# Float16 halves for the last v product, with a power of two for each token, and the last weights decoded on four engines

## The chip, the cores and the metric

The kernel runs on one core of a Trainium2 chip. The metric is the time of one execution on the device in microseconds (us). Engines are named as in the profile: PE is TensorE (PEld its weight loads), DVE is VectorE, ACT is ScalarE, POOL is GpSimd, SP is SyncE, which issues the DMAs.

## The reference, cut to what matters

Three stages follow one another over 8 batches of 576 tokens with 512 features: a linear attention, a Fourier mixing with a feed-forward network (the main part below), and a channel mixing with its own weights (the last part). The change concerns the last one:

```python
xk = mu_k * x + (1.0 - mu_k) * x_prev      # x_prev: the token before, zeros at a batch's start
xr = mu_r * x + (1.0 - mu_r) * x_prev
k = np.maximum(xk @ w_k, 0.0)              # 512 -> 1024
v = k * k @ w_v                            # 1024 -> 512
r = 1.0 / (1.0 + np.exp(-(xr @ w_r)))      # 512 -> 512
return (r * v).astype(np.float32)
```

The weights come in as float64, in pairs of 32-bit words.

## The kernel before, in words

**Products in halves.** An operand of a large matmul is split into a high and a low part, and a product is three matmuls into one PSUM bank: high by high, high by low, low by high. In most products the parts are float16, scaled by powers of two; in the v product of the last part they are fp32r (32 bits).

**Main part (loop at L896 and on).** The 4608 tokens go in nine blocks of 512. For each of 16 slices f of the hidden layer, `mm1` makes 12 matmuls into one of two `h` banks (L913), ACT takes relu into `hh` (L918), DVE the rest into `hl` (L919), and `mm2`, two slices behind, adds 12 matmuls into four `acc` banks (L933). Between the matmuls `side()` advances generators: attention, the transform and the normalisation of later blocks, and, when these have ended, `last_strand`.

**Preparing the last weights (`last_weights`, L670).** w_r, w_k and w_v are read in pieces of 128x256 float64 numbers (`load_weight`, L150, issued on SP into three `raw` buffers). A first pass over w_r and w_k (24 pieces) finds each matrix's largest magnitude: ACT takes the absolute value of the upper 16 bits (L694), DVE the maximum (L695). Then a reduction over the partitions on POOL (L698) and a few tiny DVE operations give a power of two for each matrix. The second pass goes over all 40 pieces: `decode` (L153) puts float32 numbers together from the words, in three DVE operations (L157 to L159, two `dec` buffers), ACT writes the high part and DVE the low one (L724, L725 for w_r and w_k, float16; L727, L728 for w_v, fp32r). w_v goes first.

**The last part (L963 and on).** For each of nine blocks: r = 4 x 12 matmuls with the mixed tokens as weights (L975), a sigmoid on ACT (L976); then for each of 8 slices f `mmk` makes 12 matmuls (L986), k squared is made in four operations (ACT L990, DVE L991, ACT L992, DVE L993), and `mmv`, two slices behind (three in the last block), adds 12 matmuls into four `acc` banks (L1001). At the end DVE multiplies the sigmoid with the sums (L1022) and SP stores. `mix` (L766) makes the mixed tokens of the next block meanwhile, on ACT and DVE (L781 to L787), after `bound` (L745) has found a scale for the block from its largest value.

**What sets the order.** Each engine runs its instructions in a fixed order, and so does each DMA queue. The order is set when the program is built: a planner walks the written program, with earlier lines first where two could start, and starts in its own time line whatever is ready and has a buffer. So work written late can stand early in a queue: in the profile the first `bound` runs at 870 us, beside block 6 of the main part, though its lines come after that of the last weights.

Of the kernel before, what the change touches and what calls it, by code (L numbers as in the profile page):

```python
# [45 lines left out]
def net(ctx, tc, q, k, v, w1, w2, mu_k, mu_r, w_k, w_v, w_r, ce_d, se_d, cs_d, ss_d, alt_d, id_d, out):  # L46
    nc = tc.nc
# [622 lines left out]
    def last_weights():  # L670

        wp = W["pool"] = back_pools.enter_context(tc.tile_pool(name="wp", bufs=1))
        ts = nc.vector.tensor_scalar
# [4 lines left out]

        top = wp.tile([128, 4], F32, name="top")
        am = wp.tile([128, 2, 16], F32, name="am")  # L680
# [4 lines left out]
        nc.vector.tensor_reduce(out=top[:, 2:3], in_=ab[:, :, 0], axis=AX.XY, op=ALU.max)  # L685
# [11 lines left out]
        nc.vector.tensor_reduce(out=top[:, 0:2], in_=am, axis=AX.X, op=ALU.max)  # L697
        nc.gpsimd.partition_all_reduce(out_ap=top[:, 0:3], in_ap=top[:, 0:3], channels=128, reduce_op=bass_isa.ReduceOp.max)  # L698
        yield 0
        W["top"] = top  # L700

        pw = W["pw"] = wp.tile([128, 4], F32, name="pw")
        scaled = False
        for name, src, nt, n in (plan[2], plan[0], plan[1]):
            f16 = name != "wv"
            if f16 and not scaled:
                m, inv, big_ = pw[:, 0:2], pw[:, 2:4], top[:, 0:2]
                mi, ii, bi = m.bitcast(U32), inv.bitcast(U32), big_.bitcast(U32)
                ts(out=big_, in0=big_, scalar1=LEAST, scalar2=None, op0=ALU.max)
                ts(out=mi, in0=bi, scalar1=3, scalar2=0x3F800000, op0=ALU.logical_shift_left, op1=ALU.bitwise_and)  # L710
                nc.vector.scalar_tensor_tensor(out=mi, in0=bi, scalar=0x40000000, in1=mi, op0=ALU.bitwise_and, op1=ALU.bitwise_or)
                ts(out=ii, in0=mi, scalar1=0x7F800000, scalar2=None, op0=ALU.bitwise_xor)
                ts(out=inv, in0=inv, scalar1=2.0 ** 11, scalar2=None, op0=ALU.mult)
                scaled = True
            h = wp.tile([128, nt, n], F16 if f16 else F32R, name=name + "h")
            l = wp.tile([128, nt, n], F16 if f16 else F32R, name=name + "l")
            W[name] = h, l
            for t in range(nt):
                for c in range(n // 256):
                    cs = slice(256 * c, 256 * c + 256)  # L720
                    x = decode(wp, load_weight(wp, src, t, c, RAW))
                    if f16:
                        s = pw[:, 2 + (name == "wk"):3 + (name == "wk")]
                        nc.scalar.activation(out=h[:, t, cs], in_=x, func=AF.Copy, scale=s)  # L724
                        nc.vector.scalar_tensor_tensor(out=l[:, t, cs], in0=x, scalar=s, in1=h[:, t, cs], op0=ALU.mult, op1=ALU.subtract)  # L725
                    else:
                        nc.scalar.activation(out=h[:, t, cs], in_=x, func=AF.Copy)  # L727
                        nc.vector.tensor_tensor(out=l[:, t, cs], in0=x, in1=h[:, t, cs].bitcast(F32), op=ALU.subtract)  # L728
                    yield 0
# [15 lines left out]
    def bound(i):  # L745
# [11 lines left out]
        ts(out=z[:, 1:2], in0=z[:, 0:1], scalar1=W["top"][:, 2:3], scalar2=LEAST, op0=ALU.mult, op1=ALU.max)  # L757
# [201 lines left out]
    kk = big.tile([128, 2, 4, 512], F32R, tag="w1h", name="kk")  # L959
# [176 lines left out]
```

## Time and profile before

| what | us |
|---|---|
| median of 3 runs | 1589.28 |
| lowest and highest run | 1588.1, 1591.85 |
| the profiled execution | 1591.17 |
| its span, first to last instruction | 1589.4 |
| scans of the last weights (L694) | 873 to 904 |
| decodes of the last weights (L157) | 904 to 1001 |
| the last part's matmuls | 1104.4 to 1585.6 |

PE is busy 93% of the span, DVE 58%, ACT 38%, POOL 10%. In the rows below, a group of instructions stands with its line, engine, operation, "out<-in" tiles, shapes and count; then busy time in us and the mean time of one in ns; then the engine's idle time in front of them and what ended it. "acc", "h" and "side" are PSUM banks.

### The profile page before, as it was taken

How to read it: one execution, taken by the hardware profiler on the slowest of the kernel's cores; microseconds unless marked ns; L12 is line 12 of the kernel's file. 1: busy time of each engine (PE TensorE's matmuls, PEld its weight loads, DVE VectorE, ACT ScalarE, POOL GpSimd, SP SyncE). 2: the span in 40 equal slices, each digit the busy share in tenths (PEclk: the TensorE clock that was granted, in tenths of full speed). 3: DMA queues.
4: the chain of work that ended last, by engine and by line, in shares of the span. 5: the costliest groups of instructions: out<-in, count | busy, mean ns of one | idle time of the engine just before them, and what ended most of it. 6: DMA issues, size and time to landing. Idle time of an engine off the chain costs nothing.

```text
span 1589.4 us, 18119 instructions
## 1 busy us (share of the span) xinstructions
PE 1470.3 (93%) x7072; PEld 827.7 (52%) x7072; DVE 926.5 (58%) x1680; ACT 598.1 (38%) x1034; POOL 163.6 (10%) x121
## 2 busy tenths in 40 slices
PE   4647795899999999999999889999999999999999
PEld 3534553554555555555555334444555655565555
DVE  5898977636647557465463698531455445444532
ACT  4555543323223333232232433321444334433532
POOL 0034432211020010110100120000000000000000
PEclk9878997899999999999999999999999999999999
DMA  9834422101202011011010533100011001100000
GB/s 358 298 126 172 149 99 73 47 2 46 73 23 82 16 47 59 16 48 59 15 53 20 174 126 113 47 27 27 27 54 53 27 27 53 54 27 27 27 27 27
DMA packets 44867, 112.30 MB, mean 71 GB/s; under 512 B 5708, under 2 KB 12013, under 8 KB 43757
## 3 DMA queue, kind: packets, MB, share of 16 engines
q1 hardware_dynamic: 44780, 111.14, 20.0%
q8 instruction: 55, 0.90, 0.2%
q14 instruction: 32, 0.25, 0.0%
HBM read 92.25 MB, written 18.87 MB: 70 GB/s over the span
## 4 chain that ended last, share of the span: by engine, by line
PE 74%; DVE 15%; DMA 5%; issue 2%; ACT 2%; POOL 2%; SPq 0%; DVEq 0%; ACTq 0%; POOLq 0%
PE acc L933 17%; PE h L913 17%; PE acc L1001 13%; PE h L986 12%; PE h L975 6%; DMA raw<-in_w_k_dram 3%; PE side L495 2%; PE side L515 2%; DMA raw<-in_w_dram 1%; PE side L416 1%; DVE words L239 1%; PE side L363 1%; DVE hl L919 1%; DVE dec L159 1%; DVE m L322 1%
## 5 line engine op out<-in xcount | busy, mean ns | idle before, releaser
L913 PE MATMUL h<-unh,w1h 128*128 128x512 f16 (+1 forms) x608 | 226.3, 373 | 14.0 <-DVE hl L919 8.6
L913 PE MATMUL h<-unh,w1l 128*128 128x512 f16 (+1 forms) x608 | 224.5, 371 | 5.3 <-POOL w1l L257 5.3
L913 PE MATMUL h<-unl,w1h 128*128 128x512 f16 (+1 forms) x608 | 225.9, 372 | 1.2 <-DVE unl L658 1.2
L933 PE MATMUL acc<-hl,w2h 128*128 128x512 f16 x576 | 219.3, 381 | 2.6 <-DVE hl L919 2.6
L933 PE MATMUL acc<-hh,w2l 128*128 128x512 f16 x576 | 219.3, 381 | 0.0
L933 PE MATMUL acc<-hh,w2h 128*128 128x512 f16 x576 | 212.1, 382 | 4.3 <-ACT hh L918 4.3
L1001 PE MATMUL acc<-wvh,kk 128*128 128x512 f32 x576 | 202.9, 416 | 0.0
L913 PEld LDWEIGHTS <-w1h 128*128 128x128 f16 x1216 | 118.6, 99 | 145.1 <-issue 17.2
L919 DVE SCALAR_TENSOR_TENSOR hl<-h,hh 128x512 f16<-128x512 f32 x144 | 98.9, 688 | 157.7 <-ACT hh L918 156.7
L933 PEld LDWEIGHTS <-w2h 128*128 128x128 f16 x1152 | 111.9, 98 | 136.1 <-issue 6.9
L986 PE MATMUL h<-x,wkh 128*128 128x512 f16 x576 | 173.0, 380 | 0.0
L918 ACT ACTIVATE hh<-h 128x512 f16<-128x512 f32 x144 | 84.9, 591 | 192.3 <-PE h L913 192.1
L991 DVE SCALAR_TENSOR_TENSOR ke<-h,ke 128x512 f32<-128x512 f32 x72 | 49.6, 688 | 141.9 <-ACT ke L990 141.9
L1001 PEld LDWEIGHTS acc<-wvh,kk 128*128 128x128 f32 x576 | 108.6, 189 | 30.1
L1001 PE MATMUL acc<-wvl,kk 128*128 128x512 f32 x288 | 113.5, 394 | 0.0
L986 PE MATMUL h<-x,wkl 128*128 128x512 f16 x288 | 109.2, 379 | 0.0
L990 ACT ACTIVATE ke<-h,z 128x512 f32<-128x512 f32 x72 | 49.2, 683 | 140.8 <-PE h L986 140.8
L913 PEld LDWEIGHTS <-w1l 128*128 128x128 f16 x608 | 59.9, 99 | 72.3 <-POOL w1l L257 7.3
L933 PEld LDWEIGHTS <-w2l 128*128 128x128 f16 x576 | 56.6, 98 | 67.3 <-issue 4.9
L986 PEld LDWEIGHTS <-wkh 128*128 128x128 f16 x576 | 52.7, 98 | 70.5 <-issue 14.0
L975 PE MATMUL h<-wrh,x 128*128 128x512 f16 x288 | 88.6, 380 | 0.0
L787 DVE TENSOR_TENSOR x<-aa,x 128x512 f16<-128x512 f32 x72 | 47.9, 686 | 61.0 <-PE h L975 52.4
(330 smaller groups left out, 2251.4 us busy)
## 6 DMA issues: line engine op xcount, KB each, us to landing
raw<-in_w_dram SPq DMA_DIRECT2D x22, 512.0 KB, 3.9
vt<-in_v_dram SPq DMA_DIRECT2D x16, 650.0 KB, 5.2
kt<-in_k_dram SPq DMA_DIRECT2D x16, 576.0 KB, 4.0
qt<-in_q_dram SPq DMA_DIRECT2D x16, 576.0 KB, 4.2
out_dram<-oo SPq DMA_DIRECT2D x36, 256.0 KB, 2.1
y<-yT SPq DMA_DIRECT2D x8, 1026.0 KB, 5.0
w2h<-in_w_dram SPq DMA_DIRECT2D x8, 1024.0 KB, 6.8
w2l<-in_w_dram SPq DMA_DIRECT2D x8, 1024.0 KB, 8.5
```

What stands on the lines that cost most here:

```text
L495: mm(out=pt, lhsT=a[:, e, g, js], rhs=c[:, g, :], start=first, stop=(e == 1 and g == 1 and a is el))
L515: mm(out=pt, lhsT=a[:, i, cols], rhs=c[:, i, :], start=(i == 0 and c is ch and a is yh), stop=False)
L787: nc.vector.tensor_tensor(out=l[:, t, 0:n], in0=a, in1=h[:, t, 0:n], op=ALU.subtract)
L913: mm(out=pt[:, o:o + m], lhsT=a[:, t, fs], rhs=c[:, t, o:o + m], start=(t == 0 and a is w1h and c is xh), stop=(t == 3 and a is w1l))
L918: nc.scalar.activation(out=hh[:, 0:n], in_=pt[:, 0:n], func=AF.Relu)
L919: nc.vector.scalar_tensor_tensor(out=hl[:, 0:n], in0=pt[:, 0:n], scalar=0.0, in1=hh[:, 0:n], op0=ALU.max, op1=ALU.subtract)
L933: mm(out=acc[x][:, 0:n], lhsT=a[:, f, xs], rhs=c[:, 0:n], start=(f == 0 and a is w2h and c is hh), stop=(f == NF - 1 and a is w2l))
L975: mm(out=pt[0:m, :], lhsT=a[:, t, o:o + m], rhs=c[:, t, :], start=(t == 0 and a is rh and c is wrh), stop=(t == 3 and a is rl))
L986: mm(out=pt[:, 0:n], lhsT=a[:, t, fs], rhs=c[:, t, 0:n], start=(t == 0 and a is wkh and c is kh), stop=(t == 3 and a is wkl))
L990: nc.scalar.activation(out=kr[:, 0:n], in_=pt[:, 0:n], func=AF.Relu, scale=z[:, 5:6])
L991: nc.vector.scalar_tensor_tensor(out=kr[:, 0:n], in0=pt[:, 0:n], scalar=0.0, in1=kr[:, 0:n], op0=ALU.max, op1=ALU.mult)
L1001: mm(out=acc[x][0:m, :], lhsT=a[:, o:o + m], rhs=c[:, f, :], start=(f == 0 and a is h2 and c is wvh), stop=(f == NFK - 1 and a is l2))
```

## The change

1. In `decode`, ACT shifts the low word down by 29 bits (a multiplication by 2^-29, in place), DVE does two operations in place of three, and POOL adds the two.
2. w_v is scanned as well (16 pieces more in the first pass), gets a power of two, becomes float16, and is decoded last. A `yield` more stands between decoding and splitting.
3. `mix` for k adds up the squares of the mixed tokens (four ACT squares, two POOL adds, one DVE operation into bf16). `token_scale`, after the second of the four r groups, adds them over the partitions with one matmul of a ones matrix, and makes from the sum a power of two for each token, `G`, and its inverse `rb`. `token_descale`, behind the first k group, turns `rb` by four matmuls of one column, and gives a factor for each token, `dd`.
4. k squared: DVE relu times `G`, ACT square, ACT copy to float16, DVE the rest in float16. The last multiply also takes `dd`.
5. The two halves of a mixed tile lie in one tile. For k these alternate between two places.

```diff
@@ decode
+        nc.scalar.activation(out=lo, in_=lo, func=AF.Copy, scale=2.0 ** -29)
         nc.vector.tensor_scalar(out=x, in0=hi, scalar1=3, scalar2=0x3FFFFFFF, op0=ALU.logical_shift_left, op1=ALU.bitwise_and)
-        nc.vector.scalar_tensor_tensor(out=x, in0=lo, scalar=29, in1=x, op0=ALU.logical_shift_right, op1=ALU.bitwise_or)
         nc.vector.scalar_tensor_tensor(out=x, in0=hi, scalar=0xC0000000, in1=x, op0=ALU.bitwise_and, op1=ALU.bitwise_or)
+        nc.gpsimd.tensor_tensor(out=x, in0=x, in1=lo, op=ALU.add)
@@ last_weights
-        for w, (name, src, nt, n) in enumerate(plan[0:2]):
+        for w, (name, src, nt, n) in enumerate(plan):
...
+        ones_ = W["onesb"] = wp.tile([128, 128], BF16, name="onesb")
+        nc.vector.memset(ones_, 1.0)
...
-        for name, src, nt, n in (plan[2], plan[0], plan[1]):
...
+        for w, (name, src, nt, n) in enumerate(plan):
+            h = wp.tile([128, nt, n], F16, name=name + "h")
+            l = wp.tile([128, nt, n], F16, name=name + "l")
...
                     x = decode(wp, load_weight(wp, src, t, c, RAW))
...
+                    yield 0
+                    s = pw[:, 3 + w:4 + w]
+                    nc.scalar.activation(out=h[:, t, cs], in_=x, func=AF.Copy, scale=s)
+                    nc.vector.scalar_tensor_tensor(out=l[:, t, cs], in0=x, scalar=s, in1=h[:, t, cs], op0=ALU.mult, op1=ALU.subtract)
                     yield 0
@@ mix
         if w == 1:
-            h, l = (up.tile([128, 4, 512], F16, tag="u", name="x") for _ in range(2))
+            hl = up.tile([128, 2, 4, 512], F16, tag="u", name="x")
         else:
-            h, l = (hp.tile([128, 4, 512], F16, tag=x, name="x") for x in ("sq", "d"))
+            hl = hp.tile([128, 2, 4, 512], F16, tag=("sq", "d")[i % 2], name="x")
...
+            if w == 0:
+                nc.scalar.activation(out=s2[:, min(t, 1), 0:n], in_=h[:, t, 0:n], func=AF.Square)
+                if 0 < t < 3:
+                    nc.gpsimd.tensor_tensor(out=s2[:, 0, 0:n], in0=s2[:, 0, 0:n], in1=s2[:, 1, 0:n], op=ALU.add)
+                elif t == 3:
+                    nc.vector.scalar_tensor_tensor(out=sb[:, 0:n], in0=s2[:, 1, 0:n], scalar=2.0 ** -43, in1=s2[:, 0, 0:n], op0=ALU.max, op1=ALU.add)
...
+    def token_scale(i):
...
+        pt = bank("side", 2)
+        mm(out=pt[:, 0:n], lhsT=W["onesb"], rhs=SQ[i][:, 0:n], start=True, stop=True)
...
+        nc.vector.tensor_scalar(out=rg[:, 0, 0:n], in0=pt[:, 0:n].bitcast(U32), scalar1=1, scalar2=0x3F800000, op0=ALU.logical_shift_right, op1=ALU.bitwise_and)
+        nc.vector.tensor_scalar(out=rg[:, 1, 0:n], in0=rg[:, 0, 0:n], scalar1=0x7F800000, scalar2=None, op0=ALU.bitwise_xor)
+        nc.scalar.activation(out=rb[:, 0:n], in_=rg[:, 0, 0:n].bitcast(F32), func=AF.Copy)
+        return rg[:, 1].bitcast(F32), rb
+
+    def token_descale(i, rb, subs):
...
+        for x, (o, m) in enumerate(subs):
+            mm(out=pt[0:m, x:x + 1], lhsT=rb[:, o:o + m], rhs=W["onesb"][:, 0:1], start=True, stop=True)
...
@@ the last part
-    kk = big.tile([128, 2, 4, 512], F32R, tag="w1h", name="kk")
+    kk = big.tile([128, 2, 4, 512], F16, tag="w1h", name="kk")
...
+            if x == 1:
+                G, rb = token_scale(i)
...
-            nc.scalar.activation(out=kr[:, 0:n], in_=pt[:, 0:n], func=AF.Relu, scale=z[:, 5:6])
-            nc.vector.scalar_tensor_tensor(out=kr[:, 0:n], in0=pt[:, 0:n], scalar=0.0, in1=kr[:, 0:n], op0=ALU.max, op1=ALU.mult)
+            nc.vector.scalar_tensor_tensor(out=kr[:, 0:n], in0=pt[:, 0:n], scalar=0.0, in1=G[:, 0:n], op0=ALU.max, op1=ALU.mult)
+            nc.scalar.activation(out=kr[:, 0:n], in_=kr[:, 0:n], func=AF.Square, scale=2.0 ** -76)
             nc.scalar.activation(out=h2[:, 0:n], in_=kr[:, 0:n], func=AF.Copy)
-            nc.vector.tensor_tensor(out=l2[:, 0:n], in0=kr[:, 0:n], in1=h2[:, 0:n].bitcast(F32), op=ALU.subtract)
+            nc.vector.tensor_tensor(out=l2[:, 0:n], in0=kr[:, 0:n], in1=h2[:, 0:n], op=ALU.subtract)
...
             mmk(f)
+            if f == 0:
+                dd = token_descale(i, rb, subs)
...
-            nc.vector.tensor_tensor(out=r[0:m], in0=E[0:m, x, :], in1=acc[x][0:m, :], op=ALU.mult)
+            nc.vector.scalar_tensor_tensor(out=r[0:m], in0=acc[x][0:m, :], scalar=dd[0:m, x:x + 1], in1=E[0:m, x, :], op0=ALU.mult, op1=ALU.mult)
```

## Rows read from the trace of the kernel before

**Rows 1.** The page, busy us (share of the span) x instructions of each engine.

```profile
PE 1470.3 (93%) x7072; PEld 827.7 (52%) x7072; DVE 926.5 (58%) x1680; ACT 598.1 (38%) x1034; POOL 163.6 (10%) x121
```

**Rows 2.** Busy us by stretch: length, engines (x instructions), granted clock, DMA share, GB/s.

```profile
870.00:1104.39 234.39, 220.56 (x998) 98.53 (x997) 141.87 (x346) 74.40 (x143) 14.45 (x11) 0.99 0.27 86
...
904.00:926.00 22.00, 17.11 (x70) 7.04 (x69) 19.48 (x53) 6.56 (x16) 4.72 (x3) 0.92 0.29 97
926.00:966.00 40.00, 35.77 (x157) 15.94 (x156) 39.29 (x89) 17.05 (x33) 4.34 (x2) 0.96 0.38 125
...
1159.19:1212.65 53.46, 53.46 (x241) 31.55 (x240) 26.77 (x52) 22.59 (x36) 0.64 (x1) 1.00 0.11 40
```

**Rows 3.** Chain that ended last, in order of time: start us, us, what.

```profile
1096.62 7.77 PE acc L933 x36
1104.39 10.36 PE h L975 x48
...
1122.52 2.79 PE acc L1001 x12
1125.32 2.61 PE h L986 x12
...
1176.04 2.77 PE acc L1001 x12
...
1574.42 11.17 PE acc L1001 x48
```

**Rows 4.** Waits, 840 to 1104: who waited for whom, us, times, longest.

```profile
ACT hw L694 <- DMA raw<-in_w_k_dram: 10.9, 11, 2.4
...
PE h L913 <- DVE hl L919: 6.4, 5, 2.9
...
PE acc L933 <- ACT hh L918: 3.6, 3, 2.2
```

**Rows 5.** Groups of instructions, one block of the last part, 1159.19 to 1212.65.

```profile
L986 PEld LDWEIGHTS <-wkh 128*128 128x128 f16 x64 | 5.9, 98 | 7.9 <-issue 1.6
L991 DVE SCALAR_TENSOR_TENSOR ke<-h,ke 128x512 f32<-128x512 f32 x8 | 5.5, 689 | 14.2 <-ACT ke L990 14.2
L990 ACT ACTIVATE ke<-h,z 128x512 f32<-128x512 f32 x8 | 5.5, 683 | 15.4 <-PE h L986 15.4
L993 DVE TENSOR_TENSOR kk<-ke,kk 128x512 fp32r<-128x512 f32 x8 | 5.4, 688 | 2.8 <-ACT kk L992 2.8
...
L992 ACT ACTIVATE kk<-ke 128x512 fp32r<-128x512 f32 x8 | 5.0, 628 | 3.7 <-DVE ke L991 3.7
```

**Rows 6.** Groups of instructions of POOL, whole span.

```profile
L611 POOL TENSOR_TENSOR sq<-sq 128x512 f32<-128x512 f32 x8 | 10.2, 1272 | 0.6
...
L592 POOL TENSOR_TENSOR sq<-u 128x256 f32<-128x256 f32 x2 | 1.9, 940 | 33.2 <-DVE u L537 31.0 <-PE side L575 2.2
```

**Rows 7.** Tile raw, 868 to 1010: ns min/median/max, first and last start.

```profile
L157 DVE TENSOR_SCALAR dec<-raw x40: 279/288/296, 904.4 to 1000.5; 128x256 uint32<-128x256 uint32 x40
L158 DVE SCALAR_TENSOR_TENSOR dec<-raw,dec x40: 409/417/426, 905.0 to 1001.1; 128x256 uint32<-128x256 uint32 x40
L159 DVE SCALAR_TENSOR_TENSOR dec<-raw,dec x40: 409/417/1969, 906.2 to 1001.5; 128x256 uint32<-128x256 uint32 x40
...
L694 ACT ACTIVATE hw<-raw x24: 417/432/442, 873.2 to 903.7; 128x256 bf16<-128x256 bf16 x24
```

**Rows 8.** Groups of instructions, 860 to 1104.

```profile
L695 DVE TENSOR_SCALAR_CACHE_REDUCE hw<-hw 128x256 bf16<-128x256 bf16 x24 | 10.0, 418 | 14.3 <-ACT hw L694 14.3
...
L725 DVE SCALAR_TENSOR_TENSOR wkl<-dec,pw,wkh 128x256 f16<-128x256 f32 x16 | 7.6, 478 | 0.6 <-ACT wkh L724 0.6
```

**Rows 9.** Timeline of all engines, 120 to 130: start us, us, instruction.

```profile
120.59 0.41 DVE L238 TENSOR_SCALAR words<-words 128x512 uint32<-128x512 uint32 x1
...
128.43 1.18 POOL L257 TENSOR_TENSOR w2l<-words,w2h 128x512 f16<-128x512 f32 x1 [3.02 <-ACT w2h L256]
128.51 1.38 DVE L238 TENSOR_SCALAR dec<-raw 128x512 uint32<-128x512 uint32 x1
```

More of the change, by code (lines that the diff above doesn't have):

```diff
@@ L677, in last_weights @@
         ts(out=W["mu"][:, :, 1], in0=W["mu"][:, :, 0], scalar1=-1.0, scalar2=1.0, op0=ALU.mult, op1=ALU.add)
-        top = wp.tile([128, 4], F32, name="top")
-        am = wp.tile([128, 2, 16], F32, name="am")
+        top = W["top"] = wp.tile([128, 4], F32, name="top")
+        am = wp.tile([128, 3, 16], F32, name="am")
         nc.gpsimd.memset(am, 0.0)
@@ L684, in last_weights @@
         nc.vector.tensor_tensor(out=ab[:, :, 0], in0=ab[:, :, 0], in1=ab[:, :, 1], op=ALU.add)
-        nc.vector.tensor_reduce(out=top[:, 2:3], in_=ab[:, :, 0], axis=AX.XY, op=ALU.max)
+        nc.vector.tensor_reduce(out=top[:, 3:4], in_=ab[:, :, 0], axis=AX.XY, op=ALU.max)
         yield 0
         plan = (("wr", w_r, 4, DM), ("wk", w_k, 4, FK), ("wv", w_v, NFK, DM))
-        for w, (name, src, nt, n) in enumerate(plan[0:2]):
+        for w, (name, src, nt, n) in enumerate(plan):
             for t in range(nt):
@@ L696, in last_weights @@
                     yield 0
-        nc.vector.tensor_reduce(out=top[:, 0:2], in_=am, axis=AX.X, op=ALU.max)
-        nc.gpsimd.partition_all_reduce(out_ap=top[:, 0:3], in_ap=top[:, 0:3], channels=128, reduce_op=bass_isa.ReduceOp.max)
+        nc.vector.tensor_reduce(out=top[:, 0:3], in_=am, axis=AX.X, op=ALU.max)
+        nc.gpsimd.partition_all_reduce(out_ap=top, in_ap=top, channels=128, reduce_op=bass_isa.ReduceOp.max)
+        ones_ = W["onesb"] = wp.tile([128, 128], BF16, name="onesb")
+        nc.vector.memset(ones_, 1.0)
@@ L699, in last_weights @@
         yield 0
-        W["top"] = top
-        pw = W["pw"] = wp.tile([128, 4], F32, name="pw")
-        scaled = False
-        for name, src, nt, n in (plan[2], plan[0], plan[1]):
[L705 to L716, printed above, removed]
+        pw = W["pw"] = wp.tile([128, 8], F32, name="pw")
@@ new lines, in last_weights @@
+        m, inv, big_ = pw[:, 0:3], pw[:, 3:6], top[:, 0:3]
+        mi, ii, bi = m.bitcast(U32), inv.bitcast(U32), big_.bitcast(U32)
+        ts(out=big_, in0=big_, scalar1=LEAST, scalar2=None, op0=ALU.max)
+        ts(out=mi, in0=bi, scalar1=3, scalar2=0x3F800000, op0=ALU.logical_shift_left, op1=ALU.bitwise_and)
+        nc.vector.scalar_tensor_tensor(out=mi, in0=bi, scalar=0x40000000, in1=mi, op0=ALU.bitwise_and, op1=ALU.bitwise_or)
+        ts(out=ii, in0=mi, scalar1=0x7F800000, scalar2=None, op0=ALU.bitwise_xor)
@@ L721, in last_weights @@
                     x = decode(wp, load_weight(wp, src, t, c, RAW))
[L722 to L728, printed above, removed]
+                    yield 0
+                    s = pw[:, 3 + w:4 + w]
+                    nc.scalar.activation(out=h[:, t, cs], in_=x, func=AF.Copy, scale=s)
+                    nc.vector.scalar_tensor_tensor(out=l[:, t, cs], in0=x, scalar=s, in1=h[:, t, cs], op0=ALU.mult, op1=ALU.subtract)
                     yield 0
@@ L756, in bound @@
         zi = z.bitcast(U32)
-        ts(out=z[:, 1:2], in0=z[:, 0:1], scalar1=W["top"][:, 2:3], scalar2=LEAST, op0=ALU.mult, op1=ALU.max)
+        ts(out=z[:, 1:2], in0=z[:, 0:1], scalar1=W["top"][:, 3:4], scalar2=LEAST, op0=ALU.mult, op1=ALU.max)
         ts(out=zi[:, 1:2], in0=zi[:, 1:2], scalar1=0x7F800000, scalar2=None, op0=ALU.bitwise_and)
@@ L762, in bound @@
         ts(out=z[:, 3:5], in0=W["pw"][:, 0:2], scalar1=z[:, 1:2], scalar2=2.0 ** -25, op0=ALU.mult, op1=ALU.mult)
-        nc.vector.tensor_tensor(out=z[:, 5:6], in0=z[:, 4:5], in1=z[:, 4:5], op=ALU.mult)
         yield 0
+    SQ = {}
     def mix(i, w):
@@ L787, in mix @@
             nc.vector.tensor_tensor(out=l[:, t, 0:n], in0=a, in1=h[:, t, 0:n], op=ALU.subtract)
-            yield 0
+            if w == 0:
[4 more added lines that the diff above has]
+                    nc.vector.scalar_tensor_tensor(out=sb[:, 0:n], in0=s2[:, 1, 0:n], scalar=2.0 ** -43, in1=s2[:, 0, 0:n], op0=ALU.max, op1=ALU.add)
+            yield 0
+    def token_scale(i):
+        n = blocks[i][1]
+        pt = bank("side", 2)
+        mm(out=pt[:, 0:n], lhsT=W["onesb"], rhs=SQ[i][:, 0:n], start=True, stop=True)
+        rg = W["pool"].tile([128, 2, 512], U32, tag="rg", name="rg", bufs=2)
+        rb = W["pool"].tile([128, 512], BF16, tag="rb", name="rb", bufs=1)
+        nc.vector.tensor_scalar(out=rg[:, 0, 0:n], in0=pt[:, 0:n].bitcast(U32), scalar1=1, scalar2=0x3F800000, op0=ALU.logical_shift_right, op1=ALU.bitwise_and)
[3 more added lines that the diff above has]
+    def token_descale(i, rb, subs):
+        z = SC[i][0]
+        pt = bank("side", 2)
+        for x, (o, m) in enumerate(subs):
+            mm(out=pt[0:m, x:x + 1], lhsT=rb[:, o:o + m], rhs=W["onesb"][:, 0:1], start=True, stop=True)
+        dd = W["pool"].tile([128, 2, 4], F32, tag="dd", name="dd", bufs=2)
+        nc.vector.tensor_scalar(out=dd[:, 0], in0=pt[:, 0:4], scalar1=z[:, 4:5], scalar2=2.0 ** 68, op0=ALU.mult, op1=ALU.mult)
+        nc.vector.scalar_tensor_tensor(out=dd[:, 1], in0=dd[:, 0], scalar=W["pw"][:, 6:7], in1=dd[:, 0], op0=ALU.mult, op1=ALU.mult)
+        return dd[:, 1]
     front_left = [3]
```

5 lines of the change are left out of this document (added).

## The prediction

> **What bounds the kernel now.** I read four views, in this order. The page's busy times first: TensorE (PE) is busy 93% of the span, every other engine under 60% [rows 1]. Then busy time by stretch, to find where the missing 7% lies, beside the stage that the change touches. In a whole block of the last part PE is busy 53.46 of 53.46 us, at full clock: that part ends when PE's work ends, and only a shorter PE stream shortens it. While the last weights are prepared (870 to 1104 us) PE stands idle 234.39 - 220.56 = 13.83 us, 4.89 of it between 904 and 926 and 4.23 between 926 and 966 [rows 2]; the clock of 0.99 there takes some 2 us more. Third, the chain of waits in order of time, for the price of a matmul: 36 float16 matmuls of the main part take 7.77 us and twelve of the k product 2.61 (216 to 217 ns each), twelve fp32r ones of the v product 2.79, in most groups 2.77 (231 ns) [rows 3]. Last, the waits of PE in the weight stage: it waits for hl of VectorE (DVE) and hh of ScalarE (ACT) [rows 4], work of the main part that stands behind weight work in queues whose order was fixed at build time.
>
> **The last part, step by step.** PE runs there from 1104.39 to 1574.42 + 11.17 = 1585.59 us [rows 3], 481.2 us for 9 x 240 matmuls. At the float16 price of the main part, 7.77 / 36 = 215.8 ns, 2160 matmuls take 466.2 us: **-15.0 us**. Added to PE in each block: the matmul of ones with the squares, 0.216 us as any with 512 columns, and four matmuls of one column, which hide no weight load; I take the load's 98 ns for each [rows 5], 0.4 us. No matmul of one column stands in the trace: between nothing and the 0.216 us of a whole one lie 0 and 0.86 us. So 0.61 us x 9 = **+5.5 us** (1.9 to 9.7), and the part gives **-9.5 us** (-13.1 to -5.3). By the Trainium skill, "TensorE: Matmul & The Clock Gate", section "Back-to-back issue gap", so small a matmul takes about 60 cycles, 25 ns, which as an estimate would make this -12.2; no row here shows it.
>
> What else the part gets lies beside PE. The evacuation of a k group was ACT 683, DVE 689, ACT 628, DVE 688 ns [rows 5] and becomes DVE, ACT, ACT, DVE of the same sizes: 2.7 us again. At a block's start three k groups run before the first v group, so the first evacuation has 2 x 2.61 = 5.2 us and nothing waits; without that cover 2.7 us would stand open once a block. New in a block: on DVE two passes over the token scale, one for the squares' sum and two tiny ones, about 2.3 us on top of 26.77 busy of 53.46; on ACT four squares and a copy, 5 x 0.63 = 3.1 us on 22.59 [rows 2, 5]; on POOL two adds of 128x512, 1.27 us each [rows 6]. All have half a block of idle time. The last multiply of the program is a scalar_tensor_tensor instead of a tensor_tensor, under 0.1 us.
>
> New waits on PE: the matmul of ones waits for the squares (24 r matmuls stand behind it), the four small ones for the scale's bf16 copy, and DVE's first evacuation waits for the scale. The squares come from the next block's mix; its tiles now alternate, so that mix no longer waits for the last k matmul of the block before, and has most of a block. The scale has 24 r matmuls and one k group, 7.8 us, for three passes under 0.7 us. I charge nothing; one microsecond of it in each block would be 9 us.
>
> **The weight stage, step by step.** *Scan.* 16 more loads, one ACT abs (432 ns) and one DVE max (418 ns) for each [rows 7, 8]. Scans came every (903.7 - 873.2) / 23 = 1.33 us [rows 7] and ACT waited 10.9 us for the 16 loads of w_k, 0.68 each [rows 4]: the scan is bound by its three load buffers, so it grows by 16 x 1.33 = 21 us, to about 925. On SP that is 16 more issues; behind them are stores that the last part reads much later. *Decode.* Of 40 pieces each loses one DVE pass of 417 ns and keeps 288 + 417 + 478 = 1.18 us where it had 1.60 [rows 7, 8]: DVE loses 16.7 us and gets 16 x 0.42 = 6.7 for the scans. ACT gets a pass of some 0.43 us for each piece (17 us), POOL an add over 256 columns: 0.64 us if it is half of 1.27 at 512, 0.94 by the one row of that width [rows 6], so 26 to 38 us. w_v now needs the scale and comes last; its first use is at 1122.52 [rows 3], and decoding from 925 on ends near 1021 if its rate, (1000.5 - 904.4) / 39 = 2.46 us a piece [rows 7], holds.
>
> *What PE sees of this.* Now 24 scans and 40 decodes cost PE 13.83 us, 0.216 each; 16 scans more at that mean are **+3.5 us** (ends: 0, if decodes that leave 904 to 926 cost PE there as much as scans will, and 10.9, if all of ACT's added waiting for loads reaches it). The decode itself I take as **0**: DVE loses 0.42 us a piece, but POOL's add holds it up. A DVE pass from SBUF that takes 0.41 us alone took 1.38 when it started beside a POOL pass of 1.18, and ended 0.28 after it [rows 9]. If half the adds meet such a pass, 0.32 of the 0.42 us are gone. Ends: -9.1 - 2 (all idle time of 904 to 966 and the clock's loss go) and 26 - 16.7 = +9 (every add at 0.64 us held DVE up).
>
> **Sum.** -9.5 + 3.5 = -6.0 us. The profiled execution took 1591.17 us around its span of 1589.4, 1.9 over the median of 1589.28; the difference holds for both, so the median should become **1583.3 us**. About 0.2%, 3.2 us, is what a measurement of this kernel tells from no change.
>
> **Rivals.**
> *A: the stalls melt, 1568 us.* From 904 to 926 the queues hold scans (0.42 us of DVE each) instead of decodes (1.6 us), just where the normalisation of the last block also needs DVE. For it: 9.12 of the 13.83 us idle lie there [rows 2]. Then the stage gives -9.1 - 2 - 1 for the decodes after it, 12 us, with nothing for the scans: 1589.3 - 9.5 - 12 = 1568. Against it: the scan phase had waits on loads of its own.
> *B: POOL in the chain, slower, 1596 us.* Every piece now goes ACT, DVE, POOL, ACT, DVE, with two decode buffers and three load buffers, and the load buffer is held until POOL has added. hh and hl of the main part stand in the ACT and DVE queues between these steps, so when a piece takes longer than the fixed order supposes, PE waits for them. Price: 40 adds of 0.94 us less the 16.7 removed are +21, of which I take 13, and 3.5 for the scans: -9.5 + 16.5 = +7. It decides from (9.5 + 3.2 - 3.5) / 40 = 0.23 us a piece that reaches PE. For it: rows 9, and the waits in rows 4; against it: an unread PSUM bank leaves PE three groups, 7.8 us, before it must wait. A sentence of the Trainium skill is of B's kind: the "GPSIMD Engine Reference", section "Engine selection", advises VectorE for elementwise adds, GpSimd being about twice as slow with two inputs, and its "Key points" name contention on shared SBUF interfaces with VectorE; the trace agrees with 1.38 against 0.41 us [rows 9].
> *C: the last part gains nothing, 1592 us.* Either PE waits about 1 us in each block for the squares or the scale, or the v product keeps its 231 ns in float16, and the new matmuls come on top. Against it: PE never waits there now, and the k and r products show the float16 price on the same PE. With a wait of 9 us: 1589.3 - 9.5 + 9 + 3.5 = 1592; with the old price of v it would be 1589.3 + 5.5 + 3.5 = 1598.
>
> **How the numbers follow.** My forecast (1577 to 1590) gets 0.42, A 0.25, B 0.23, C 0.10. Faster by over 0.2%: A and four fifths of the forecast, 0.59. Slower by over 0.2%: most of B and a third of C, 0.22. The rest, 0.19, is the same. The range takes A and B with their middles and the bounds of the small matmuls: 1566 to 1599; the forecast's own is 1577 to 1590.
>
> **What the next profile would show.** Right: groups of twelve v matmuls at 2.59 to 2.62 us in the chain, a block of 52.3 to 52.7 us with PE busy throughout, no PE wait on the squares or the scale; scans until about 925 and decodes to about 1020; PE idle between 870 and the last part of about 17 us. A shows as under 5 us there, B as 25 us or more, with DVE passes next to POOL's adds near 1 us and hh or hl late. A block over 53 us would mean C. I would be wrong altogether if the fixed order of the queues changed elsewhere, in the first 800 us, which the change does not touch, or if the mix of the first block were late, so that PE waits at the start of the last part.

## The result, and the profile after

The changed kernel takes 1605.87 us (median of 4 runs, 1605.23 to 1607.3) against 1589.06 for the kernel before on the same chip: a ratio of **1.0104, 95% interval 1.0087 to 1.0122**, some 17 us slower. Forecast were 1583.3 us, and a range that ended at 1599. The profiled execution took 1606.08 us, its span is 1604.3.

First the chain of waits around the start and at the end of the last part, in order of time (start us, us, what), beside [rows 3]:

```profile
1120.95 7.77 PE acc L964 x36
1128.72 5.18 PE h L1006 x24
...
1147.26 2.59 PE acc L1034 x12
1149.85 2.59 PE h L1019 x12
...
1590.08 10.37 PE acc L1034 x48
```

Twelve v matmuls take 2.59 us where they took 2.77 to 2.79. The last part lasts from 1128.72 to 1590.08 + 10.37 = 1600.45, 471.7 us where it was 481.2: the 9.5 us of the forecast. But it **starts 24.3 us later** (it started at 1104.39). All of the loss lies ahead of it. Busy time by stretch, columns as in [rows 2]:

```profile
1186.69:1239.34 52.65, 52.28 (x246) 23.68 (x246) 30.54 (x56) 24.94 (x42) 3.65 (x3) 1.00 0.11 40
870.00:1128.72 258.72, 225.70 (x993) 99.38 (x992) 161.26 (x371) 111.60 (x224) 56.24 (x54) 0.95 0.31 98
904.00:926.00 22.00, 15.28 (x60) 6.29 (x60) 16.33 (x45) 8.76 (x21) 4.86 (x3) 0.92 0.60 194
926.00:966.00 40.00, 31.82 (x128) 13.64 (x128) 29.90 (x72) 20.24 (x41) 13.77 (x15) 0.87 0.36 111
1000.00:1022.00 22.00, 12.87 (x53) 5.37 (x52) 12.20 (x29) 6.73 (x14) 4.38 (x6) 0.77 0.16 53
```

While the last weights are prepared PE is idle 258.72 - 225.70 = 33.0 us (it was 13.8), at a granted clock of 0.95 (it was 0.99). 9.1 us of that lie between 1000 and 1022, where DVE and ACT are idle too, so no engine was short of time there. The waits of 840 to 1129 (who waited for whom, us, times, longest; [rows 4]) lead to POOL:

```profile
ACT wkh L724 <- POOL dec L160: 17.6, 5, 11.2
PE h L944 <- DVE hl L950: 17.0, 5, 9.1
POOL dec L160 <- issue: 16.7, 4, 7.2
...
PE acc L964 <- ACT hh L949: 12.5, 4, 5.7
```

PE waits for evictions as before, but behind them ACT now waits for POOL's add, once for 11.2 us, and POOL waits for "issue", which is nothing that the profile sees another engine hold. POOL's timeline shows what stands there:

```profile
925.34 0.39 POOL L699 PARTITION_ALL_REDUCE top<-top  x1 [14.08 <-DVE top L698]
932.67 1.42 POOL L160 TENSOR_TENSOR dec<-dec,raw 128x256 uint32<-128x256 uint32 x2 [6.95 <-issue]
...
997.41 0.73 POOL L160 TENSOR_TENSOR dec<-dec,raw 128x256 uint32<-128x256 uint32 x1 [1.17 <-DVE dec L159]
1004.69 0.38 POOL L751 PARTITION_ALL_REDUCE z<-z  x1 [6.55 <-issue]
1012.22 1.41 POOL L160 TENSOR_TENSOR dec<-dec,raw 128x256 uint32<-128x256 uint32 x2 [7.16 <-issue]
```

Each time POOL goes from adds to an all-reduce or back, it does nothing for 6.55 to 7.16 us. One all-reduce, that of block 1's largest value, lies in the middle of the decode: 14.1 us without an add, of which 3.5 pass before DVE has that value ready (999.40 + 2.28 = 1001.68). DVE and PE in turn (timeline):

```profile
999.40 2.28 DVE L750 TENSOR_REDUCE z<-y 128x1 f32<-128x2052 f32 x1
...
1013.51 0.48 DVE L725 SCALAR_TENSOR_TENSOR wkl<-dec,pw,wkh 128x256 f16<-128x256 f32 x1 [7.55 <-ACT wkh L724]
...
1016.90 0.68 DVE L950 SCALAR_TENSOR_TENSOR hl<-h,hh 128x512 f16<-128x512 f32 x1
```
```profile
1017.63 0.58 PE L944 MATMUL h<-unh,w1h 128*128 128x512 f16 x1 [9.13 <-DVE hl L950]
1018.01 0.63 PE L944 MATMUL h<-unl,w1h 128*128 128x512 f16 x1
1018.44 0.63 PE L944 MATMUL h<-unh,w1l 128*128 128x512 f16 x1
...
1021.18 0.38 PE L944 MATMUL h<-unh,w1h 128*128 128x512 f16 x1
```

An eviction (hl) stands in DVE's queue behind a low part that waits for the add; PE stands 9.13 us, and then starts a matmul every 0.43 us instead of every 0.216, at the lower of its two levels (1.2 GHz), until about 1020.9; the clock granted in that stretch is 0.77 on average.

In the kernel before the all-reduce of block 1 came at 1044.25, after the decode, whose pieces POOL had no part in. Why it moved, SP's timelines show: the load of block 1's y was issued at 1036.83 before, and is issued at 993.32 now (two lines of before, one of the changed kernel).

```profile
1036.83 0.37 SPq L743 DMA_DIRECT2D y<-yT  x1
1044.25 0.38 POOL L754 PARTITION_ALL_REDUCE z<-z  x1 [100.35 <-DVE z L753]
```
```profile
993.32 0.38 SPq L740 DMA_DIRECT2D y<-yT  x1
```

The mixed tokens of r lie in one buffer of the tag "u" where they took two (part 5 of the change), so a buffer is free earlier, and the planner, which starts what is ready, put the load, the maximum and the all-reduce among the decodes. They did not come alone: the mixing of block 0 moved into the decode as well. DVE's passes for the low part of x (tile x, 900 to 1050) in the kernel before and in the changed one:

```profile
L787 DVE TENSOR_TENSOR x<-aa,x x8: 680/684/692, 1026.0 to 1037.8; 128x512 f16<-128x512 f32 x8
```
```profile
L788 DVE TENSOR_TENSOR x<-aa,x x8: 678/679/1758, 973.9 to 996.3; 128x512 f16<-128x512 f32 x8
```

The scans and decodes by their tile (ns min/median/max, first and last start; [rows 7]):

```profile
L695 ACT ACTIVATE hw<-raw x40: 413/433/441, 872.0 to 924.1; 128x256 bf16<-128x256 bf16 x40
L158 DVE TENSOR_SCALAR dec<-raw x40: 276/292/1239, 925.1 to 1040.9; 128x256 uint32<-128x256 uint32 x40
...
L160 POOL TENSOR_TENSOR dec<-dec,raw x40: 718/736/3262, 932.7 to 1043.0; 128x256 uint32<-128x256 uint32 x40
```

Scans end at 924, as forecast; decodes at 1043 and not at 1021, and 14 of those 22 us are the hole.

### The profile page after: what moved, and what is told of

The parts are those of the page before. It is cut to its first block, busy times and chain, and to the rows that moved or that the text cites. A ratio compares the mean times of both kernels' runs of the same rounds, so it can differ in the third digit from the quotient of the medians.

```text
span 1604.3 us, 18533 instructions
## 1 busy us (share of the span) xinstructions
PE 1467.8 (91%) x7115; PEld 760.2 (47%) x7117; DVE 962.5 (60%) x1710; ACT 642.5 (40%) x1135; POOL 226.0 (14%) x179
## 5 line engine op out<-in xcount | busy, mean ns | idle before, releaser
L1034 PE MATMUL acc<-wvh,kk 128*128 128x512 f16 x576 | 181.4, 379 | 0.0
L964 PEld LDWEIGHTS <-w2h 128*128 128x128 f16 x1152 | 112.2, 99 | 145.8 <-issue 14.1
L1034 PEld LDWEIGHTS <-kk 128*128 128x128 f16 x864 | 84.5, 98 | 102.0
L1024 ACT ACTIVATE ke<-ke 128x512 f32<-128x512 f32 x72 | 45.1, 626 | 184.8 <-DVE ke L1023 184.8
L1023 DVE SCALAR_TENSOR_TENSOR ke<-h,rg 128x512 f32<-128x512 f32 x72 | 49.6, 689 | 113.3 <-PE h L1019 113.1
L1034 PE MATMUL acc<-wvl,kk 128*128 128x512 f16 x288 | 109.2, 379 | 0.0
L1026 DVE TENSOR_TENSOR kk<-ke,kk 128x512 f16<-128x512 f32 x72 | 49.7, 691 | 67.4 <-ACT kk L1025 66.7
```

The source lines that it names most:

```text
L964: mm(out=acc[x][:, 0:n], lhsT=a[:, f, xs], rhs=c[:, 0:n], start=(f == 0 and a is w2h and c is hh), stop=(f == NF - 1 and a is w2l))
L1024: nc.scalar.activation(out=kr[:, 0:n], in_=kr[:, 0:n], func=AF.Square, scale=2.0 ** -76)
L1034: mm(out=acc[x][0:m, :], lhsT=a[:, o:o + m], rhs=c[:, f, :], start=(f == 0 and a is h2 and c is wvh), stop=(f == NFK - 1 and a is l2))
```

## The experiments

Three theories at the start: **R**, POOL's change between all-reduce and add is what costs; **L**, the longer chain of every piece (rival B as it was written); **S**, the 16 scans. Ratios are to the kernel before on the same chip (its medians there were 1590.8 to 1593.4 us). "Last part from" is the start of the first matmul with w_r in the trace, which is 1104.23 in the kernel before and 1128.55 in the changed one.

| run | ratio, 95% interval | last part from |
|---|---|---|
| e1_reduce_behind_adds | 1.0076 (1.0061 to 1.0091) | 1125.66 |
| e2_decode_as_before | 0.9995 (0.9986 to 1.0004) | 1113.24 |
| e3_decode_alone | 1.0098 (1.0083 to 1.0113) | 1120.41 |
| e4_reduce_on_pe | 0.9992 (0.9982 to 1.0001) | 1110.90 |
| e5_or_on_dve | 1.0020 (1.0008 to 1.0032) | 1115.81 |
| e6_reduce_by_dma | 1.0577 (1.0559 to 1.0596) | 1145.58 |
| e7_no_v_scan | 0.9923 (0.9908 to 0.9938) | 1101.51 |
| e8_decode_later | 1.0102 (1.0087 to 1.0117) | 1129.72 |
| e9_z_on_pe | 1.0034 (1.0017 to 1.0050) | 1117.15 |
| e10_old_decode_pe_max | 0.9928 (0.9910 to 0.9946) | 1103.63 |
| e11_v_scan_late | 0.9978 (0.9969 to 0.9988) | 1110.93 |
| e12_r_two_buffers | 1.0009 (1.0000 to 1.0019) | 1119.43 |
| e13_y_behind_decode | 0.9979 (0.9970 to 0.9988) | 1111.84 |
| e14_pe_max_r_two | **0.9917** (0.9903 to 0.9930) | 1101.95 |
| e15_old_decode_r_two | 0.9961 (0.9947 to 0.9975) | 1110.85 |
| e16_no_v_scan_r_two | 0.9921 (0.9904 to 0.9937) | 1104.69 |
| e17_or_on_dve_r_two | 0.9989 (0.9979 to 0.9998) | 1115.05 |
| e18_late_top | 0.9957 (0.9942 to 0.9972) | 1110.67 |

### One part at a time

**e1: the all-reduce behind the last add.**

```diff
+        with (tc.issue_after(LAST[0].ins) if i else ExitStack()):
             nc.gpsimd.partition_all_reduce(out_ap=z[:, 0:1], in_ap=z[:, 0:1], ...)
```

> The changed kernel, with the maximum across partitions of block 1 (and later blocks) queued on POOL behind the last add of the decode, so that POOL changes from all-reduce to add once and not twice inside the weight stage. Theory R (POOL pays some 7 us each time it changes between an all-reduce and an add, and PE waits for the piece that stands behind it): the two gaps of 6.55 and 7.16 us in the middle of the decode go, PE's wait of 9.13 us and the half clock behind it with them; 1592 to 1596 us, which is 10 to 14 us less than the changed kernel. Theory L (the four-engine decode is a longer chain for every piece, and DVE and POOL hold each other up): the pieces keep their length, 1603 to 1608 us. Theory S (the 16 scans of w_v push the whole decode back): 1603 to 1608 us too.

1.0076, 4 us of the 10 to 14: R's number was missed. POOL's timeline, then DVE's:

```profile
1033.58 0.74 POOL L160 TENSOR_TENSOR dec<-dec,raw 128x256 uint32<-128x256 uint32 x1 [1.71 <-ACT unh L659]
1040.08 0.38 POOL L753 PARTITION_ALL_REDUCE z<-z  x1 [5.77 <-issue]
```
```profile
1040.49 0.21 DVE L756 TENSOR_SCALAR z<-z,top 128x1 f32<-128x1 f32 x1 [5.03 <-POOL z L753]
```

The edit moved only POOL's instruction. The switch is still there, and DVE, which reads the result, now waits for it instead. So e1 decides nothing between R and L; what is to be moved is the whole chain of block 1.

**e2: the decode of before**, with the float16 products and the scans of the change.

```diff
-        nc.scalar.activation(out=lo, in_=lo, func=AF.Copy, scale=2.0 ** -29)
+        nc.vector.scalar_tensor_tensor(out=x, in0=lo, scalar=29, in1=x, op0=ALU.logical_shift_right, op1=ALU.bitwise_or)
-        nc.gpsimd.tensor_tensor(out=x, in0=x, in1=lo, op=ALU.add)
```

> The changed kernel with the decode of before (three operations on DVE, nothing on ACT and POOL): the float16 v products and the scans of w_v alone. POOL has no add between its all-reduces. Theory R: last part 9.5 us shorter, scans a few us; 1580 to 1587 us. Theory L: the same 1580 to 1587 us, since the chain of a piece is the old one. Theory S (the scans are what costs): 1593 us or more, because they are still there.

0.9995: the four-engine decode carries the whole loss of 17 us, but what is left is no gain. The result lies between R's and S's numbers, so something else costs more than forecast as well; e7 shows below that it is the scans.

**e3: the four-engine decode alone**, the mirror image, in the kernel before.

> The kernel before with the four-engine decode alone (v products in fp32r, no scan of w_v). Block 1's all-reduce stands behind the decode here, as it did before, so one change of POOL from all-reduce to add is left, ahead of the first piece. Theory R: 1589 to 1597 us (nothing to one gap of 7 us). Theory L (a longer chain in each of 40 pieces, from 0.23 us a piece on): 1600 us or more.

1.0098, in L's range. But my reading of R, that one switch would be left, was wrong. POOL's timeline:

```profile
904.67 1.15 POOL L160 TENSOR_TENSOR dec<-dec,raw 128x256 uint32<-128x256 uint32 x1 [16.01 <-DVE top L698]
912.42 0.38 POOL L699 PARTITION_ALL_REDUCE top<-top  x1 [6.60 <-issue]
920.28 0.73 POOL L160 TENSOR_TENSOR dec<-dec,raw 128x256 uint32<-128x256 uint32 x1 [7.48 <-issue]
```

Here w_v needs no scale, so its first adds come before the weights' maximum, and two switches stand in the chain; PE has waits of 10.87 and 4.88 us right there. The run doesn't separate R from L.

**e4: both maxima over the partitions on TensorE.**

```diff
-        nc.gpsimd.partition_all_reduce(out_ap=top, in_ap=top, ...)
+        for x in range(4):
+            ts(out=dg[:, x, :], in0=idt, scalar1=top[:, x:x + 1], scalar2=None, op0=ALU.mult)
+        mm(out=pt, lhsT=one1, rhs=dg.rearrange("p x c -> p (x c)"), start=True, stop=True)
+        nc.vector.tensor_reduce(out=top, in_=pt.rearrange("p (x c) -> p x c", x=4), axis=AX.X, op=ALU.max)
```

(z in the same way.)

> The changed kernel with both maxima across partitions made by TensorE (a diagonal matrix with the values, times ones, then a maximum on DVE) in place of POOL's all-reduce; POOL's adds stay. POOL runs no all-reduce in the weight stage and changes nothing. Theory R: all three gaps go, 14 to 21 us less than the changed kernel, 1585 to 1592 us. Theory L: 1602 to 1608 us, the adds and shifts are all still there. Theory S: 1602 to 1608 us.

0.9992: with all adds still on POOL the loss is gone, against L and S. Only, the matmul for the weights' maximum stood late in PE's queue, and most of the decode ran from 1000 to 1095 instead of 925 to 1043. So the place could be the reason, theory **P**.

### Reload, hop, or place

**e5: an OR on DVE in place of POOL's add** (ACT's shift stays).

> The changed kernel with the last step of a piece's decode as an OR on DVE in place of the add on POOL; ACT's shift stays, so a piece is ACT, three operations of DVE, ACT, DVE, and POOL is not in it. Theory R (the pieces stand behind POOL's change between all-reduce and add): 1.000 of the kernel before (0.997 to 1.003), as with the whole decode of before. Theory A (ACT's shift, 40 of 0.43 us in ACT's queue ahead of the evictions, is what makes PE wait): 1.007 or more.

1.0020, 13 us better than the changed kernel. The decode lies in the same place (925.8 to 1039), and so do block 0's mixing (from 969.9) and block 1's all-reduce (1001.06): POOL's add is what costs here. **e6: the maxima by way of DRAM.**

> The changed kernel with both maxima across partitions by way of DRAM (write the 128 values, read them back to every partition, maximum on DVE); the adds of the decode stay on POOL and POOL has no all-reduce, and unlike the run with TensorE's reduction the decode need not move. Theory R (the change of POOL's code is the cost): 1.000 to 1.004 of the kernel before. Theory P (the run with TensorE's reduction was good because its decode lay 70 us later, from 1000 to 1095, where DVE and ACT have little else): the decode lies at 925 to 1040 again, and the time is 1.007 to 1.011.

1.0577. The waits of 850 to 1250 tell why:

```profile
DVE z L759 <- DMA zb<-zd: 50.2, 5, 12.1
```

Reading the values back keeps DVE, in its fixed order, up to 12 us at a time, in the last part too; a new wait took the place of the old one and the run says nothing on R. **e8: the decode later**, by 44 empty steps.

> The changed kernel with 44 empty steps between the reduction of the scans and the decode, so that the decode comes some 60 us later in the program; all-reduces and adds on POOL stay as they are. Theory R: the reloads of POOL come with it, 1.006 to 1.011 of the kernel before. Theory P (place alone): 0.998 to 1.002, as with TensorE's reduction.

1.0102, but the edit did not move the decode (weights' all-reduce at 923.67, against 925.34): P was not tried by it, and the run is in effect the changed kernel once more (1.0104).

**e9: only z on TensorE**, the weights' maximum on POOL. The decode stays in its place.

> The changed kernel with block maxima (z) made by TensorE and the weights' maximum (top) left on POOL; the adds stay on POOL and the decode stays where it is, at 925 to 1040. One reload is left, ahead of the first add. Theory R: the 14 us hole in the middle of the decode goes, 1.001 to 1.005 of the kernel before. Theory L (the hop over POOL in each of 40 pieces is the cost): 1.008 to 1.011.

1.0034, in R's range: the hole went, the hop over POOL stayed. But more went with it: the load of block 1's y is at 1039.04 here, and block 0's mixing behind the decode (from 1044.4), so the run does not take out the all-reduce alone. **e12: r's tokens in two buffers again.**

```diff
-            hl = up.tile([128, 2, 4, 512], F16, tag="u", name="x")
+            h, l = (up.tile([128, 4, 512], F16, tag="u", name="x") for _ in range(2))
```

> The changed kernel with the parts of r's x in two buffers again, as before, in place of one. The load of y of block 1 then has to wait for a buffer, and block 1's maximum with it. Theory R: the all-reduce falls behind the decode, as in the kernel before, and the 14 us hole goes; 1.001 to 1.005. If the all-reduce stays within the decode: 1.008 to 1.011.

1.0009, just under R's range. The whole change but for this one allocation, and 15 us of the 17 are gone (11.8 by the spans of the two traces). POOL's timeline:

```profile
928.19 0.52 POOL L699 PARTITION_ALL_REDUCE top<-top  x1 [14.44 <-DMA raw<-in_w_r_dram]
935.83 1.42 POOL L160 TENSOR_TENSOR dec<-dec,raw 128x256 uint32<-128x256 uint32 x2 [7.12 <-issue]
...
1062.23 0.38 POOL L751 PARTITION_ALL_REDUCE z<-z  x1 [5.90 <-issue]
```

y of block 1 is loaded at 1053.47, and its all-reduce lies behind the decode; one switch is left, ahead of the first add. Block 0's mixing lies behind the decode too (tile x, 900 to 1062):

```profile
L788 DVE TENSOR_TENSOR x<-aa,x x8: 673/684/693, 1041.5 to 1054.5; 128x512 f16<-128x512 f32 x8
```

So the root is shown: a buffer that came free early let foreign work in among the pieces. But e12 does not say how much of the 15 us is the all-reduce and how much the mixing. Pairs without POOL's add tell: there one buffer in place of two costs 5.4 us (e2 against e15, below) and 4.9 (e5 against e17). And POOL's add costs 13.4 us with one buffer (the changed kernel against e5), 3.2 with two (e12 against e17). So some 5 of the 15 us come without any add on POOL, and some 10 only with its adds. That is close to the sum of PE's wait of 9.13 us and the 1.6 us that eight matmuls at the lower clock take longer. No run takes out the all-reduce alone.

### The scans, and the rest of the decode

**e7: no scans of w_v**, with the decode of before (the scale from w_k's largest value).

> The changed kernel with the decode of before and without the 16 scans of w_v (its scale is taken from w_k's largest value, which leaves out the largest value of w_v). Theory S (the scans are why the float16 products with the old decode bring 0.05% and not 0.6%): 0.994 to 0.997 of the kernel before. Rival: the scans lie beside other work, and the loss comes from the work on x and its squares that the decode now collides with; 0.998 to 1.001.

0.9923, beyond S's range: against e2 the scans cost 0.0072, 11.5 us. Busy time of e2, then of e7:

```profile
900.00:960.00 60.00, 48.74 (x201) 20.69 (x199) 47.30 (x124) 23.77 (x49) 9.23 (x5) 0.91 0.49 153
960.00:1000.00 40.00, 36.01 (x165) 16.00 (x164) 37.06 (x84) 21.15 (x39) 4.23 (x3) 1.00 0.35 106
1000.00:1060.00 60.00, 57.65 (x262) 25.63 (x263) 53.25 (x131) 28.40 (x54) 3.21 (x3) 0.97 0.31 102
```
```profile
900.00:960.00 60.00, 50.57 (x216) 21.81 (x214) 50.02 (x123) 21.04 (x41) 8.36 (x5) 0.94 0.36 108
960.00:1000.00 40.00, 38.41 (x177) 17.17 (x176) 39.95 (x101) 23.46 (x43) 3.13 (x3) 1.00 0.35 113
1000.00:1060.00 60.00, 60.00 (x280) 27.20 (x278) 42.76 (x92) 25.64 (x46) 3.41 (x3) 1.00 0.20 65
```

Where the scans lie, PE loses 1.8 us of work and 0.03 of its clock over 60 us, 1.8 more: 3.6, the forecast's term. The larger part, 2.4 + 2.35 us and again 1.8 by the clock, is lost after 960, where the decode of e2 lasts until 1037 and that of e7 until 1013, beside the work on x. Two attempts to get that half back: **e11**, w_v's scans behind the decode of w_r and w_k, and **e13**, meant to load block 0's y behind the last decode.

> The changed kernel with the decode of before, and with the 16 scans of w_v and their maximum moved behind the decode of w_r and w_k. Theory S1 (the scans cost 11 us where they lie, at 900 to 925, beside the last work of the first part; later, DVE and ACT are idle for 70 us): 0.992 to 0.996 of the kernel before. Theory S2 (16 more pieces cost the same wherever they lie): 0.998 to 1.001.

> The changed kernel with the decode of before, and with the load of block 0's y queued behind the last piece of the decode, so that the mixing of x and its maximum can't lie among the pieces. Theory C (the scans cost 3 us where they lie and push the decode into the work on block 0's x, where the other 6 to 8 us are lost): 0.992 to 0.997 of the kernel before. Theory S2 (the loss is in the pieces themselves): 0.998 to 1.001, or slower if x is then late for the last part.

0.9978 and 0.9979, some 2.6 us better than e2 each and short of the ranges. But e13's edit did not do what it was meant to: block 0's y is loaded at 825.75 (826.81 in e2), its mixing starts at 965.7 (966.8 in e2), and block 1's all-reduce stays at 998.33. So C was not tried; e13 is in effect e2 on another chip, and shows that two such ratios can lie 0.0016 apart. e11, which did move the scans, is no further from e2 than that: moving them gave back at most a quarter of their price, and neither of its theories holds as written. **e15 and e16** repeat the pair with r in two buffers:

> The changed kernel with the decode of before and r's x in two buffers. Against the run with two buffers alone (1.0009) it takes the shift off ACT and the add off POOL, with the all-reduce of block 1 outside the decode in both: the price of the four-engine decode without the hole. Theory R (the four-engine decode costs only its reloads; one is left ahead of the first add): 0.995 to 0.999. Theory L (it costs some 0.23 us or more in each of 40 pieces besides): 0.991 to 0.995.

> The changed kernel with the decode of before and r's x in two buffers, without the 16 scans of w_v (its scale from w_k's largest value, which leaves out w_v's). Against the same with the scans (0.9961). If the scans cost what the forecast gave them, once block 1's all-reduce is out of the decode: 0.993 to 0.995. If they cost 11 us whatever the order: 0.988 to 0.990.

0.9961 and 0.9921: here the scans cost 0.0040, 6.4 us, the last part starting 6.2 us later. That lies between e16's two ranges, its interval reaching into the first. e2, e7, e15 and e16 form a square: without the scans one buffer or two makes no difference (0.9923 and 0.9921), with them it makes 5.4 us. So 5 of the 11.5 us are neither the scans' alone nor the mixing's, but come when the scans push the decode back and the mixing lies in it too. With e12 (1.0009) e15 gives the four-engine decode without the hole: 0.0048, 7.6 us, as R had it. **e17** splits it.

> The changed kernel with r's x in two buffers and the add of the decode as an OR on DVE. It lies between the run with two buffers alone (1.0009, add on POOL) and that with the decode of before (0.9961). If the 7.6 us between them are POOL's (the reload of 7 us ahead of the first add): 0.996 to 0.998. If they are the shift's on ACT: 1.000 to 1.002.

0.9989, between its two ranges: 4.5 us for ACT's shift, 3.2 for POOL's add. By the traces the two starts of the last part say the same (4.2 and 4.4 us), and POOL's share lies at the remaining switch: PE is busy 44.86 us from 900 to 960 in e12 and 48.13 in e17, but 37.85 + 55.17 from 960 to 1060 in e12 and 36.02 + 55.38 in e17, so past the switch the hop costs no more than the OR on DVE that stands in its place. These two parts are near the width of the intervals (about 2 us each); their sum is not. The split also depends on the order: against e15, e12 has started 35 matmuls fewer between 900 and 960 (168 against 203, 7.6 us of PE's work) and only 4 fewer from 960 to 1060, so with the add on POOL all of the 7.6 us is lost before 960, around the first switch, and the shift's 4.5 us show only in e17.

### A version that beats both

**e10: the decode of before and TensorE's maxima**; **e14: the same with r in two buffers.**

> The changed kernel with the decode of before and both maxima on TensorE. If the late place of the decode (1000 to 1095 in the run with TensorE's maxima) is itself worth something, 0.992 to 0.997 of the kernel before; if only the reload counted there, 0.998 to 1.001, as with the decode of before alone.

> The best so far (the decode of before, both maxima on TensorE) with r's x in two buffers as before. Block 1's load of y then leaves the stage, as in the run with two buffers alone: 0.989 to 0.993 of the kernel before if DVE's work on block 1 still costs there, 0.992 to 0.994 if TensorE's maxima had already taken all that this edit brings.

0.9928 and 0.9917 (the two buffers' share, 0.0011, is within the intervals), 13 us faster than the kernel before and 30 than the changed one. In e14 the decode starts at 1003, but for two pieces at 926. Its busy time by stretch:

```profile
960.00:1000.00 40.00, 40.00 (x185) 18.11 (x184) 5.21 (x8) 4.18 (x7) 0.00 (x0) 1.00 0.00 1
1000.00:1060.00 60.00, 60.00 (x281) 27.39 (x279) 56.88 (x148) 30.61 (x58) 2.74 (x2) 1.00 0.40 123
1060.00:1100.00 40.00, 40.00 (x187) 18.09 (x185) 29.03 (x78) 14.03 (x27) 0.00 (x0) 1.00 0.31 99
```

PE doesn't wait once among the decodes, though DVE is busy 56.88 of 60 us. Whether that is the late place or the missing all-reduces, **e18** was to tell, with the weights' maximum on POOL but late:

> The changed kernel with the decode of before and r's x in two buffers, and with the weights' maximum left on POOL but queued behind an eviction some 60 us later, so that the decode starts at about 1000. Theory P (what TensorE's maxima brought with the old decode is the late place, where DVE and ACT have nothing but the evictions): 0.990 to 0.993 of the kernel before, as with TensorE's maxima. Theory T (it came from taking the all-reduces off POOL): 0.995 to 0.998, as without it.

0.9957, the value of e15 (0.9961); but the all-reduce came at 925.98 again, so the place was not moved, the run is in effect e15 once more, and the question stays open.

## Why the prediction was wrong

Walking from the kernel before to the changed one (1 in the ratio is 1590 us; each step after the first is one edit): the float16 products with their token scale, w_v decoded last, without scans (e16) -12.6; the scans (e15) +6.4; ACT's shift (e17) +4.5; POOL's add (e12) +3.2; r in one buffer (the changed kernel) +15.1. The sum is +16.6. In the order that the prediction used, with one buffer throughout, the same sum is -12.2 (e7), +11.5 for the scans (e2) and +17.3 for the four-engine decode (the changed kernel).

- **The last part, -9.5 (-13.1 to -5.3): right**, 471.7 us, but that it came out to the tenth is luck: two errors cancel. In e12, where PE never waits at a block's start, a block is 52.11 us from r group to r group, 1.35 under [rows 2], so nine give -12.2; the five matmuls added take some 0.3 us and not 0.61. PE's timeline of the changed kernel has the four small ones:

```profile
1191.87 0.24 PE L815 MATMUL side<-onesb,rb 128*128 128x1 bf16 x4
1191.98 0.59 PE L1019 MATMUL h<-x,wkh 128*128 128x512 f16 x2
```

  The next matmul starts 0.11 us after the first of the four, some 27 ns for each. So the Trainium skill's 25 ns ("TensorE: Matmul & The Clock Gate", section "Back-to-back issue gap") was nearer than the load's 98 ns that I took; the trace agrees with it. With r in one buffer 2.7 us of the 12.2 are lost again, to waits that I charged at nothing: PE waits up to 0.4 us for a sigmoid at the start of five blocks.
- **Scan, +3.5 (0 to 10.9): undersized**, +6.4 with two buffers and 11.5 with the changed kernel's one. The end at 925 and the loss among the scans were right; the step asked only what PE loses where the scans lie, not what the pieces they push back meet later.
- **Decode, 0 (-11 to +9): the step that failed.** It cost 17.3 us (the changed kernel against e2): 7.6 without the hole, within its bounds, and some 10 more with it. I had counted DVE's and POOL's busy time. What cost most was neither: it was two changes of POOL between add and all-reduce in the middle of the pieces. The rows for it were in the trace of before. POOL's timeline has two all-reduces of the first part with 5.81 and 7.17 us of idle time from the end of an add that is put down to "issue":

```profile
297.40 1.08 POOL L338 PARTITION_ALL_REDUCE m<-m  x1 [5.81 <-issue]
...
372.39 1.08 POOL L338 PARTITION_ALL_REDUCE m<-m  x1 [7.17 <-issue]
```

  I did not list what else stands in POOL's queue once its adds are in a chain that PE waits for. Nor did I ask what the smaller tile of part 5 sets free. Why ACT's shift costs 4.5 us in e17 is not shown.
- **Rival B had the sign and PE's idle time (25 us or more forecast, 33.0 seen), not the mechanism**: it priced a hop in each of 40 pieces, and e12 against e17 finds none past the first switch. Nor did DVE's passes grow beside POOL's: the median of the first one (L158) is 292 ns, and was 288 [rows 7]. *A* fell: from 904 to 926 PE is idle 6.7 us, more than before. *C* fell with the last part.
- The sum without the hole and the four-engine decode, -6.0, is what e15 measures (0.9961, -6.2). That is luck as well: a gain (12.6) and a price (6.4) that were both taken too small by the same 3 us.

## What to carry to other kernels

Before an engine gets a place in a chain that the critical engine waits for, list everything else in its queue there, and what each change of kind costs: on POOL an all-reduce among adds brought two idle stretches of some 7 us here. Where a planner sets the order, a change of a buffer's size is a change of the schedule; look for what may now start early. Price a piece of added work also by where it pushes its successors. And before a run is read, see in its trace whether the edit moved what it was to move: in e8, e13 and e18 it did not, and in e9 it moved more.

## What the runs showed of the hardware

In all 20 traces no all-reduce on POOL starts less than 5.5 us after the end of an add before it (the least is 5.53, in e9), and no add less than 6.7 us after an all-reduce (6.72, in e16); from add to add the time is often nothing. In the changed kernel the first piece's parts from DVE and ACT were ready at 925.9, and the add started at 932.67. The stretch ahead of an all-reduce is not work of its own that the trace fails to show: at 1044.25 in the kernel before, when POOL had been idle for 100 us, it started 0.14 us after its input was there, and took 0.38. So the change seems to begin when the work before has ended, and runs while POOL waits for its input.

The Trainium skill, "GPSIMD Engine Reference", section "Instruction dispatch", gives about 6 us for the first call of a freshly loaded kernel. The size is near that of these stretches; that they are such loads no trace shows, and here they come back with every change, in both directions. An add of 128x256 takes 0.74 us in the median, 0.64 to 0.94 having been the bounds.

The section "Engine selection" of the same page of the Trainium skill names GpSimd for a reduction along the partitions. Here a matmul with a diagonal matrix and a maximum on DVE, in its place, made the kernel 0.4 to 0.7% faster (e14 against e15, e10 against e2), with the late decode that came with it.
